# Delta-rule attention and two MoE layers on one core: GpSimd takes over five transposed copies, and the planner's costs of its inverses change

## The chip, the cores and the metric

The kernel runs on one core of a Trainium2 chip. The metric is the device time of one execution in microseconds (us); before the change the median of three runs is 900.76 us (897.88 to 901.03). TensorE is called PE, VectorE DVE, ScalarE ACT, GpSimd POOL, and SP issues the DMAs.

## The reference, cut to what matters

```python
def _attn_ref(q, k, v, beta):                    # 4 x 8 heads, 768 tokens, dim 48
    k_n = k / (np.linalg.norm(k, axis=-1, keepdims=True) + 1e-06)
    state = np.zeros((B, H, D, D))
    for t in range(S):
        y[:, :, t] = np.einsum('bhd,bhde->bhe', q[:, :, t], state)
        v_old = np.einsum('bhde,bhd->bhe', state, kt)
        state = state + bt[:, :, :, None] * np.einsum('bhd,bhe->bhde', kt, vt - v_old)
def _moe_ref(x, w_in, w_out, g_ln):              # 3072 tokens, 384 -> 1024 -> 384
    h = x @ w_in
    ...                                          # h * softmax(h), layer norm, * g_ln
    return ln @ w_out
def _moe2_ref(x, w_in, w_out):                   # 384 -> 2048 -> 384
    return (np.maximum(x @ w_in, 0.0) ** 2) @ w_out
```

The output of the attention goes through both layers.

## The kernel before, in words

The attention is computed in chunks of 64 tokens. Two chunks of eight heads each make one step t; there are 24 steps. A step needs the inverse of a unit lower triangular 64 x 64 matrix of each chunk and head. It is built from inverses of 32 x 32 blocks. The inverses of four steps (128 blocks, one on each partition) are computed together as one group, so there are six groups, g = 0 to 5 (`G0`). Group 0 is inverted on DVE, groups 1 to 5 on POOL.

The path of a group, with the lines of the profile:
- PE multiplies keys and queries (L662), ACT evicts them (L688) and SP writes them to a scratch tensor `gscr` in HBM. A chain on DVE (L790 to L799) and a small transpose on PE (L816) make the factors, which ACT evicts as `gm` (L819).
- `inversion(g, ...)` loads the blocks into a tile `it` (two of them, used in turn; order's names it_205 for odd groups and it_204 for even ones), scales them by `gm` (L891), keeps their lower triangles (L873), and then does 102 small steps: for each j a product (L910) and an addition (L927), each in one or two pieces, each depending on the one before. It ends with a memset of the diagonal (L945) and a scaling by `gm` (L952).
- `it` is written to the scratch `tscr`. A copy of it with the two block indices exchanged, `ia` (L969), is made by ACT, and written to the scratch `uscr`. From both `load_tb` fetches what a step needs.
- PE combines the blocks of step t in `prep1` (L1062, needs `tscr`) and `prep2` (L1078, needs `uscr`), and `z` (L1105), which ACT evicts as `zs` (L1119). The step itself is the products `a` (L1132, L1133), the difference r on DVE (L1148), the products `o` (L1162, L1163) and the state on DVE (L1180). `a` of step t writes the same PSUM bank as `prep1` of step t + 1 and stands behind it in PE's queue; so step 3 comes after `prep1` of step 4, the first step of group 1.
- Each step gives 128 tokens, and the first MoE layer for them fills PE's time: transposes (L1204), the first product (`p_h`, L1215), softmax and norm on DVE and ACT, transposes (`p_tr`, L1317, evicted as zh and zl, L415 and L420), and for pairs of steps the second product (`p_x`, L1337, evicted as xo, L1351). The weights are decoded from raw 64-bit words on ACT (L458, L539) and DVE (L466 to L502); the low parts `wgl` of one of them are made on POOL (L420). POOL also scales the values `vt` (L1042).
- The second MoE layer (L1480, L1524) comes last.

All queues are ordered by a planner. Every operation is recorded by `add(engine, cost, function, reads, writes, priority)`. `Plan.forward` simulates the engines with these costs and always takes, of the operations that are ready, the one with the best key; `Plan.backward` computes new keys from the same costs; the best of twelve rounds becomes the order in which the instructions are issued. Each engine executes its queue strictly in that order on the chip. A cost is a number of the planner only; it changes no instruction. `c_pool(n)` is the planner's cost of n elements on POOL, `c_act(n, True)` that of an ACT copy within SBUF: for the 1024 elements of `ia`

```python
def c_act(n, sbuf=False):
    return (0.095 if sbuf else 0.053) + n / 1200.0
```

gives 0.95 us.

Of the kernel before, what the change touches and what calls it, by code (L numbers as in the profile page):

```python
# [20 lines left out]
HB = 32  # L21
# [94 lines left out]
class Plan:  # L116
# [19 lines left out]
    def add(self, eng, cost, fn, r=(), w=(), prio=0.0, size=0, after=()):  # L136

        i = len(self.ops)
        deps = set(after)
        for k in r:  # L140
            if k in self.writer:
                deps.add(self.writer[k])
            if k in self.BANKS:

                deps.update(j for j in self.readers.get(k, ()) if self.ops[j][0] != eng)
            self.readers.setdefault(k, []).append(i)
        for k in w:
            if k in self.writer:
                deps.add(self.writer[k])
            deps.update(self.readers.get(k, ()))  # L150
            self.writer[k], self.readers[k] = i, []
        deps.discard(i)
        self.ops.append((eng, cost, fn, prio, deps, size))
        return i
# [108 lines left out]
def c_dve(n, fast=False):  # L263
    return 0.07 + n / (1920.0 if fast else 960.0)


def c_act(n, sbuf=False):
    return (0.095 if sbuf else 0.053) + n / 1200.0


def c_pool(n, full=True):

    return 0.148 + n * (2.104e-3 if full else 1.667e-3)
# [3 lines left out]
def tile_delta_moe_moe(  # L277
# [14 lines left out]
    v, act, pool, pe = nc.vector, nc.scalar, nc.gpsimd, nc.tensor  # L292
# [94 lines left out]
    ia = ap_.tile(sqr, F32, name="ia")  # L387
# [446 lines left out]

    def inversion(g, en, prio):

        eng, cost = (v, lambda n, full=True: c_dve(n) + 0.09) if en == "dve" else (pool, c_pool)
        gm = gm_[g % 2]
        it, itmp = it_[g % 2], junk[:, 512:] if g == 1 else itmp_
        kgm, kic, kia = ("A", "gm", g % 2), ("A", "itc", g % 2), ("A", "ia")  # L840
# [5 lines left out]
        n = 2 * (G0[g + 1] - G0[g])  # L846
# [54 lines left out]
        for j in range(1, HB - 1):  # L901
            nr = HB - 1 - j
            for q, (c0, c1) in enumerate(((0, min(j, s1)), (s1, j))):
                w_ = c1 - c0
                if w_ <= 0:
# [13 lines left out]
                    full=False,  # L919
# [35 lines left out]
            full=False,  # L955
# [7 lines left out]
            prio,  # L963
            P * 4096,
        )
        add(
            "act",
            c_act(HB * HB, True),
            lambda: act.copy(ia.rearrange("p s r -> p r s"), it),  # L969
            kts,  # L970
            [kia, *(kraws if g == 0 else ())],
            prio,
# [180 lines left out]
    def o_mm(t):  # L1153
        first, last = t % NCH == 0, t % NCH == NCH - 1

        def mm():
            for i in range(2):
                for p in range(NP):
                    for h in range(2):
                        s = rows[h]  # L1160
                        if not last:
                            pe.matmul(ksp[heads[h], i, p], zs_[i][s, p, C:112], R[s, i, p], start=True, stop=True)  # L1162
                        pe.matmul(  # L1163
                            xp[rows[1 - h], i, p],
                            zs_[i][s, p, 0:C],
                            R[s, i, p],
                            start=first and i == 0 and p == 0,
                            stop=True,
                            skip_group_check=True,
                        )  # L1170

        return mm, [("A", "zs", 0), ("A", "zs", 1), ("A", "r")], [("A", "a"), ("A", "o")]
# [393 lines left out]
    for t in range(T1):  # L1566
        wr = e_tile(t, -70 + t)
        norms(t, -62)
    gammas(0, -61)
    inversion(0, "dve", -55)  # L1570
    first_inv.append(plan.writer["A", "it", 0, 0])
    for t in range(T1, T2):
# [4 lines left out]

    gate.append(wr)
    inversion(1, "pool", PR["inv1"])
    load_w1i(0, 6, PR["w1i"])  # L1580
    for t in range(T2, LA):
# [16 lines left out]
    for t in range(NT + 3):  # L1598
        if t < NT:
            for g in range(2, NG):  # L1600
                if t == max(1, G0[g] - 5):
                    gammas(g, t + PR["inv"])
                    inversion(g, "pool", t + PR["inv"])
# [7 lines left out]
            parts, cost = [], 0.3  # L1611
# [23 lines left out]
            parts, cost = [o_mm(t)], 1.25  # L1635
# [113 lines left out]
```

## Time and profile before

| | |
|---|---|
| median of three runs | 900.76 us |
| profiled execution | 896.73 us |
| its span (first to last instruction) | 895.0 us |
| mean granted clock of PE (1 is 2.4 GHz, 0.5 is 1.2 GHz) | 0.96 |
| PE busy | 804.2 us (90%) |
| DVE, ACT, POOL busy | 494.7, 449.6, 311.7 us |

The span has three stages: the start until the first inverses are there, with PE often idle; the steps with the first MoE layer, to about 460 us; and the second MoE layer, where PE is busy nearly all the time. POOL works until 433 us, nearly all of it before 388 us. In a view of one engine in order of time, each line has the start, the duration of the merged instructions, the operation, and in brackets how long the engine sat idle before it and which instruction of which engine ended that.

### The profile page before, as it was taken

What the parts mean: (1) busy time and instruction counts of PE and PEld (TensorE: products, weight loads), DVE (VectorE), ACT (ScalarE), POOL (GpSimd) and SP (SyncE); (2) the same over time, 40 slices, a digit from 0 to 9 for tenths busy, and PEclk for the clock granted to TensorE, in tenths of its full rate; (3) what the DMA queues carried; (4) which work ended last, traced back from release to release, by engine and by line L of the source; (5) the groups of instructions that cost most, each with busy time, mean ns of one, the idle gap of its engine ahead of it and who ended that gap; (6) DMA issues with size and microseconds to landing.
All of it is one profiled execution on the core that took longest, in us unless ns stands there. A gap on an engine that the chain in (4) does not pass through costs nothing.

```text
span 895.0 us, 24146 instructions
## 1 busy us (share of the span) xinstructions
PE 804.2 (90%) x9904; PEld 748.0 (84%) x9904; DVE 494.7 (55%) x990; ACT 449.6 (50%) x996; POOL 311.7 (35%) x751
## 2 busy tenths in 40 slices
PE   5425759999978989999999999999999999999997
PEld 4324637888867878878889999999999999999997
DVE  5999765634974895775756444343334333343332
ACT  2315568675765675756666444343434333343333
POOL 5469989847978978920000000000000000000000
PEclk9975878999998999999999999999999999999999
DMA  9947866577687686466244311010101001010101
GB/s 243 275 119 175 251 160 172 138 158 187 176 254 190 198 204 188 145 178 182 88 130 127 112 48 53 1 54 1 53 1 38 17 1 53 1 27 1 27 1 27
DMA packets 139726, 99.71 MB, mean 111 GB/s; under 512 B 95072, under 2 KB 120672, under 8 KB 139616
## 3 DMA queue, kind: packets, MB, share of 16 engines
q1 hardware_dynamic: 139616, 98.18, 40.3%
q8 instruction: 77, 1.26, 0.6%
q14 instruction: 33, 0.27, 0.1%
HBM read 71.41 MB, written 26.74 MB: 110 GB/s over the span
## 4 chain that ended last, share of the span: by engine, by line
PE 63%; POOL 12%; DVE 7%; DMA 6%; ACT 5%; issue 3%; SPq 3%; ACTq 0%; POOLq 0%; DVEq 0%
PE acc L1524 22%; PE h L1480 22%; PE p_x L1337 7%; POOL it L927 6%; PE p_h L1215 5%; POOL junk L910 3%; SPq L300 3%; DMA raw<-in_w2i_dram 2%; POOL itmp L910 2%; PE p_tr L1317 2%; PE p_a L1132 1%; DMA m<-in_ktok_dram 1%; PE p_u L1105 1%; PE p_o L1163 1%; DVE zl L420 1%
## 5 line engine op out<-in xcount | busy, mean ns | idle before, releaser
L1501 DVE TENSOR_TENSOR xt<-xt 128x384 f32<-128x384 f32 x128 | 71.5, 558 | 167.3 <-ACT xt L1493 167.1
L1493 ACT ACTIVATE xt<-h 128x384 f32<-128x384 f32 x128 | 63.0, 492 | 167.1 <-PE h L1480 167.0
L1480 PE MATMUL h<-x1l,w2h 128*128 128x384 f32 x384 | 128.7, 335 | 0.0
L1480 PE MATMUL h<-x1h,w2h 128*128 128x384 f32 x384 | 128.6, 335 | 0.0
L1480 PE MATMUL h<-x1h,w2l 128*128 128x384 f32 x384 | 128.5, 335 | 0.0
L927 POOL TENSOR_TENSOR it<-it,itmp 128x72 f32<-128x72 f32 (+37 forms) x204 | 89.4, 454 | 4.6
L1524 PE MATMUL acc<-woh,xh 128*128 128x384 f32 x258 | 87.7, 340 | 0.7 <-ACT ot L1546 0.7
L1337 PE MATMUL p_x<-zh,wgh 128*128 128x256 f32 x288 | 86.2, 299 | 1.9 <-ACT xo L1351 1.8
L1524 PE MATMUL acc<-wol,xh 128*128 128x384 f32 x258 | 87.4, 339 | 0.0
L1524 PE MATMUL acc<-woh,xl 128*128 128x384 f32 x258 | 87.1, 338 | 0.0
L910 POOL TENSOR_TENSOR itmp<-it 128x72 f32<-128x72 f32 (+37 forms) x204 | 85.9, 436 | 2.2
L1337 PE MATMUL p_x<-zl,wgh 128*128 128x256 f32 x288 | 82.1, 285 | 0.0
L1337 PE MATMUL p_x<-zh,wgl 128*128 128x256 f32 x288 | 82.1, 285 | 0.0
L420 DVE TENSOR_TENSOR xl<-xt,xh 128x384 fp32r<-128x384 f32 x86 | 48.0, 558 | 44.7 <-ACT xh L415 44.4
L1480 PEld LDWEIGHTS h<-x1h,w2h 128*128 128x128 f32 x384 | 72.1, 188 | 0.0
L1480 PEld LDWEIGHTS h<-x1l,w2h 128*128 128x128 f32 x384 | 72.1, 188 | 0.0
L1480 PEld LDWEIGHTS h<-x1h,w2l 128*128 128x128 f32 x384 | 72.1, 188 | 0.0
L415 ACT CAST xh<-xt 128x384 fp32r<-128x384 f32 x86 | 44.1, 513 | 48.2 <-DVE xt L1501 47.0
L1215 PE MATMUL p_h<-w1h,xh 128*128 128x512 f32 x144 | 62.8, 436 | 3.3 <-DVE xl L420 3.3
L1337 PEld LDWEIGHTS p_x<-zh,wgh 128*128 128x128 f32 x288 | 55.2, 192 | 5.7 <-ACT xo L1351 2.9
L1215 PE MATMUL p_h<-w1l,xh 128*128 128x512 f32 x144 | 58.9, 409 | 0.0
L1215 PE MATMUL p_h<-w1h,xl 128*128 128x512 f32 x144 | 58.7, 408 | 0.0
(181 smaller groups left out, 1967.4 us busy)
## 6 DMA issues: line engine op xcount, KB each, us to landing
kql<-in_kin_dram SPq DMA_DIRECT2D x22, 512.0 KB, 6.5
kqe<-in_kin_dram SPq DMA_DIRECT2D x38, 192.0 KB, 6.5
raw<-in_w2i_dram SPq DMA_DIRECT2D x12, 512.0 KB, 5.2
raw<-in_w2o_dram SPq DMA_DIRECT2D x16, 384.0 KB, 4.2
gscr<-g SPq DMA_DIRECT2D x21, 256.0 KB, 4.2
m<-in_ktok_dram SPq DMA_DIRECT2D x24, 192.0 KB, 3.8
vt<-in_vtok_dram SPq DMA_DIRECT2D x24, 192.0 KB, 4.6
x1scr<-xo SPq DMA_DIRECT2D x12, 384.0 KB, 2.6
```

What stands on the lines that cost most here:

```text
L300: return add("sp", 0.06, lambda: nc.sync.dma_start(dst(), src()), r, w, prio, size, gate)
L415: add("act", c_act(n), lambda: act.copy(hi(), src()), r, [w[0]], prio)
L420: lambda: le.tensor_tensor(out=lo(), in0=src(), in1=hi().bitcast(F32), op=ALU.subtract),
L910: lambda tm=tm, j=j, nr=nr, w_=w_, c0=c0, c1=c1: eng.tensor_tensor(out=tm, in0=it[:, j + 1 :, j : j + 1].to_broadcast([P, nr, w_]), in1=it ...
L927: lambda tm=tm, j=j, c0=c0, c1=c1: eng.tensor_tensor(out=it[:, j + 1 :, c0:c1], in0=it[:, j + 1 :, c0:c1], in1=tm, op=ALU.add,),
L1215: pe.matmul(p_h[:, sl], xx[:, c], ww[:, c, sl], start=(c == 0 and k == 0), stop=(c == 2 and k == 2),)
L1317: pe.transpose(ptr[:, f], e[:, k * P : k * P + P], ident)
L1337: pe.matmul(p_x1[:, 0 : 2 * P], ww[:, f, c * P : c * P + P], zz[:, f], start=(f == 0 and k == 0), stop=(f == 7 and k == 2),)
L1480: pe.matmul(late["h2", ih], late[ww][:, c, s], xx[:, c], start=(c == 0 and k == 0), stop=(c == 2 and k == 2),)
L1493: lambda: act.activation(out=rt, in_=late["h2", ih], func=AF.Relu),
L1501: lambda: v.tensor_tensor(out=gg, in0=rt, in1=rt, op=ALU.mult),
L1524: pe.matmul(late["acc", a], gg[:, a * P : a * P + P], late[ww][:, f], start=(f == 0 and k == 0), stop=(f == 15 and k == 2),)
```

## The change

Two things. The planner reckons each step of an inverse on POOL longer: by 0.12 us in group 1, by 0.06 us in groups 2 to 5 (DVE's 0.09 us for group 0 is as before). And the copy `ia` of groups 1 to 5 is made by POOL itself (`tensor_copy`, reckoned with 1.95 us); ACT keeps that of group 0.

```diff
     def inversion(g, en, prio):
 
-        eng, cost = (v, lambda n, full=True: c_dve(n) + 0.09) if en == "dve" else (pool, c_pool)
+        eng, slow = (v, 0.09) if en == "dve" else (pool, 0.12 if g == 1 else 0.06)
+        cost = lambda n, full: (c_dve(n) if en == "dve" else c_pool(n, full)) + slow
...
+        ce, cn = (act.copy, c_act(HB * HB, True)) if g == 0 else (pool.tensor_copy, 1.95)
         add(
-            "act",
-            c_act(HB * HB, True),
-            lambda: act.copy(ia.rearrange("p s r -> p r s"), it),
+            "pool" if g else "act",
+            cn,
+            lambda: ce(ia.rearrange("p s r -> p r s"), it),
             kts,
             [kia, *(kraws if g == 0 else ())],
             prio,
```

The lines after the first edit are one further down in the changed kernel, those after the second two further (L891 is L892, L952 is L953, L969 is L971, L1062 is L1064). Because the costs feed all keys, the order changes on every engine. Three places follow.

POOL, the last steps of group 1 (it_205) and the start of group 2 (it_204). Before, from its last addition on:

```order
L927 TENSOR_TENSOR it_205<-it_205,junk 128x21
L945 MEMSET it_205 128x32
L952 TENSOR_TENSOR it_205<-it_205,gm_210 128x1024
L1042 TENSOR_TENSOR vt_189<-vt_189,nrv_185 128x384
L420 TENSOR_TENSOR wgl<-wst_217,wgh 128x384
L420 TENSOR_TENSOR wgl<-wst_218,wgh 128x384
L891 TENSOR_TENSOR it_204<-it_204,gm_209 128x1024
L873 AFFINE_SELECT it_204<-it_204 128x1024
```

Now, 24 steps before the end of group 1, and then its last rows:

```order
L928 TENSOR_TENSOR it_205<-it_205,junk 128x7x9
L941 MEMSET idle 128x16
L892 TENSOR_TENSOR it_204<-it_204,gm_209 128x1024
L911 TENSOR_TENSOR junk<-it_205 128x96
L911 TENSOR_TENSOR junk<-it_205 128x54
L928 TENSOR_TENSOR it_205<-it_205,junk 128x6x16
L928 TENSOR_TENSOR it_205<-it_205,junk 128x6x9
L941 MEMSET idle 128x16
L874 AFFINE_SELECT it_204<-it_204 128x1024
```

```order
L928 TENSOR_TENSOR it_205<-it_205,junk 128x21
L911 TENSOR_TENSOR itmp<-it_204 128x130
L946 MEMSET it_205 128x32
L928 TENSOR_TENSOR it_204<-it_204,itmp 128x26x5
L953 TENSOR_TENSOR it_205<-it_205,gm_210 128x1024
L941 MEMSET idle 128x16
L420 TENSOR_TENSOR wgl<-wst_220,wgh 128x384
L911 TENSOR_TENSOR itmp<-it_204 128x150
L971 COPY ia<-it_205 128x32x32
```

The start of group 2 (L892, which needs gm_209 from ACT, and L874) and its first ten steps now stand ahead of the end of group 1, and so do three `wgl`; the copy follows L953 with one `wgl` and one step between.

ACT, around the copy of group 1 (it_205), in the queue that also evicts z (zs_199, zs_200) and makes gm_209. Before:

```order
L1119 COPY zs_199<-p_u_221 128x448
L415 CAST xh_152<-p_h 128x384
L1258 ACTIVATE ez_157<-ez_157,sc_155 128x1024
L819 COPY gm_209<-p_u_221 128x32
L458 ACTIVATE wst_220<-raw_214 128x384
L969 COPY ia<-it_205 128x32x32
L1119 COPY zs_200<-p_u_222 128x448
```

Now:

```order
L1121 COPY zs_199<-p_u_221 128x448
L539 ACTIVATE wst_217<-wst_217,gsb 128x384
L415 CAST wgh<-wst_217 128x384
L819 COPY gm_209<-p_u_221 128x32
L539 ACTIVATE wst_218<-wst_218,gsb 128x384
L415 CAST wgh<-wst_218 128x384
L415 CAST xh_152<-p_h 128x384
L1260 ACTIVATE ez_157<-ez_157,sc_155 128x1024
L1189 COPY xt_149<-p_o 64x4x48 x4
L1121 COPY zs_200<-p_u_222 128x448
```

The copy is gone between the two evictions of z, and gm_209 stands further ahead.

POOL, the end of group 3 (it_205 again) and the start of group 4 (it_204). Before:

```order
L927 TENSOR_TENSOR it_205<-it_205,itmp 128x21
L945 MEMSET it_205 128x32
L952 TENSOR_TENSOR it_205<-it_205,gm_210 128x1024
L1042 TENSOR_TENSOR vt_189<-vt_189,nrv_184 128x384
L891 TENSOR_TENSOR it_204<-it_204,gm_209 128x1024
L873 AFFINE_SELECT it_204<-it_204 128x1024
```

Now:

```order
L928 TENSOR_TENSOR it_205<-it_205,itmp 128x21
L892 TENSOR_TENSOR it_204<-it_204,gm_209 128x1024
L946 MEMSET it_205 128x32
L874 AFFINE_SELECT it_204<-it_204 128x1024
L953 TENSOR_TENSOR it_205<-it_205,gm_210 128x1024
L911 TENSOR_TENSOR itmp<-it_204 128x30
L971 COPY ia<-it_205 128x32x32
L928 TENSOR_TENSOR it_204<-it_204,itmp 128x30
L1044 TENSOR_TENSOR vt_189<-vt_189,nrv_184 128x384
```

Here too the next group's L892 and L874 stand ahead of L953. In groups 2, 4 and 5 nothing of the next group stands ahead of L953, and the copy follows it at once or behind one vt.

On PE, between the small transpose L816 of group 2 and `prep1` of step 4, there are now 36 matmuls of `p_h` where there were 27, 24 of `p_x` where there were none, and five sets of four p_tr where there were three. Between L816 of group 4 and `prep1` of step 12, the first of group 3, there are 30 of `p_h` and 72 of `p_x` where there were 12 and 24.

## Rows read from the trace of the kernel before

**Rows 1.** The page: busy shares, and PE's busy tenths in 40 slices.

```profile
PE 804.2 (90%) x9904; PEld 748.0 (84%) x9904; DVE 494.7 (55%) x990; ACT 449.6 (50%) x996; POOL 311.7 (35%) x751
...
PE   5425759999978989999999999999999999999997
```

**Rows 2.** Windows: busy of PE, PEld, DVE, ACT, POOL; clock; DMA share; GB/s.

```profile
130.00:440.00 310.00, 288.92 (x5868) 250.76 (x5869) 206.77 (x397) 211.89 (x498) 216.55 (x567) 0.96 0.66 180
...
280.00:300.00 20.00, 19.52 (x356) 17.29 (x357) 11.10 (x19) 11.94 (x32) 17.25 (x45) 0.83 0.68 191
```

**Rows 3.** ACT in order of time, around its copies of groups 1, 3 and 5.

```profile
116.26 0.18 ACT L819 COPY gm<-p_u 128x32 f32<-128x32 f32 x1
...
123.74 1.93 ACT L969 COPY ia<-it 128x1024 f32<-128x1024 f32 x1 [6.84 <-POOL it L952]
...
255.36 0.67 ACT L458 ACTIVATE wst<-raw 128x512 f32<-128x512 f32 x1 [4.15 <-DMA raw<-in_w2i_dram]
255.99 1.96 ACT L969 COPY ia<-it 128x1024 f32<-128x1024 f32 x1
...
385.55 2.04 ACT L969 COPY ia<-it 128x1024 f32<-128x1024 f32 x1 [3.70 <-POOL it L952]
```

**Rows 4.** PE in order of time, the instructions that it waited for.

```profile
67.35 0.74 PE L1062 MATMUL p_a<-tbd,g 32*32 32x32 f32 x32 [16.41 <-DMA tbd<-tscr]
...
126.09 1.57 PE L662 MATMUL p_u<-kqe 48*64 48x128 f32 x28 [3.13 <-ACT zs L1119]
...
130.31 1.12 PE L1317 MATMUL p_tr<-ident,ez 128*128 128x128 f32 x4 [2.65 <-DVE zl L420]
...
139.27 0.65 PE L1062 MATMUL p_a<-tbd,g 32*32 32x32 f32 x32
...
258.56 0.26 PE L816 MATMUL p_u<-ident,be 32*32 32x32 f32 x8 [3.09 <-ACT zs L1119]
...
280.48 1.11 PE L1317 MATMUL p_tr<-ident,ez 128*128 128x128 f32 x4 [2.41 <-ACT ez L1258]
...
388.04 0.39 PE L1337 MATMUL p_x<-zh,wgh 128*128 128x256 f32 x1 [0.96 <-ACT xo L1351]
```

**Rows 5.** POOL in order of time: end of group 1, start of group 2.

```profile
107.03 0.88 POOL L910 TENSOR_TENSOR junk<-it 128x96 f32<-128x96 f32 x2
...
109.62 0.99 POOL L420 TENSOR_TENSOR wgl<-wst,wgh 128x384 fp32r<-128x384 f32 x1
...
117.00 3.61 POOL L927 TENSOR_TENSOR it<-it,junk 128x40 f32<-128x40 f32 x1
...
121.79 1.91 POOL L952 TENSOR_TENSOR it<-it,gm 128x1024 f32<-128x1024 f32 x1
...
128.54 2.36 POOL L891 TENSOR_TENSOR it<-it,gm 128x1024 f32<-128x1024 f32 x1
130.97 1.27 POOL L873 TENSOR_SCALAR_AFFINE_SELECT it<-it 128x1024 f32<-128x1024 f32 x1
132.32 0.25 POOL L910 TENSOR_TENSOR itmp<-it 128x30 f32<-128x30 f32 x1
...
139.62 0.66 POOL L927 TENSOR_TENSOR it<-it,itmp 128x130 f32<-128x130 f32 x1
```

**Rows 6.** DVE in order of time beside 117.00, and POOL's groups by form (busy, mean ns).

```profile
117.60 1.01 DVE L477 SCALAR_TENSOR_TENSOR wst<-wst,cst 128x384 uint32<-128x384 uint32 x2
...
L927 POOL TENSOR_TENSOR it<-it,itmp 128x40 f32<-128x40 f32 x8 | 2.5, 309 | 0.0
```

**Rows 7.** SP in order of time: from the copy of group 0 to the loads.

```profile
62.85 1.41 SPq L300 DMA_DIRECT2D uscr<-ia  x2
64.36 2.19 SPq L300 DMA_DIRECT2D tbd<-tscr  x4
```

**Rows 8.** The chain in order of time: PE's fillers.

```profile
164.72 2.88 PE p_x L1337 x24
...
170.87 2.09 PE p_h L1215 x9
```

## The prediction

> **What bounds the kernel now.** I read the page first, then windows, then each engine in order of time around the six copies `ia`. The page shows PE busy for 804.2 of 895.0 us, and its slices show where the rest is: digits of 2 to 7 at the start, mostly 9 from the seventh slice on, with an 8 or a 7 here and there [rows 1]. So the last stage can't get faster by this change, since PE alone sets it, and what the change can win or lose is PE's idle time in the first 460 us. In the 310 us from 130 to 440 PE is busy for 288.9 us; some 21 us are idle there [rows 2]. A wait costs more than itself where the clock falls: from 280 to 300 us the granted clock is 0.83 of 2.4 GHz, right behind a stall of 2.41 us at 280.48, which is 6.8 us at 1.2 GHz (0.17 / 0.5 x 20), in which PE did 3.4 us less than at 2.4 GHz [rows 2, 4].
>
> ACT in order of time shows what the copies do there. Its copy of group 1 stands in the queue from 116.9 on and waits 6.84 us for POOL, then runs 1.93 us; in group 5 it waits 3.70 us and runs 2.04 [rows 3]. All that stands behind it on ACT waits too. PE shows who feels it: at 126.09 it had waited 3.13 us for an eviction of z (zs) that stood behind the copy, and at 130.31 2.65 us for the low parts zl, which come from evictions further back in the same queue; at 258.56 it had waited 3.09 us for a zs behind the copy of group 3, and at 388.04 0.96 us for an xo behind that of group 5 [rows 3, 4]. The planner reckoned 0.95 us for a copy that takes 1.93 to 2.04, and it thought the inverses shorter than they are, so it put the copy where the chip isn't ready for it.
>
> **What the planner's numbers do.** A cost by itself runs nothing longer. What counts is the new order, and two consequences of it. First, with an inverse that ends later in the plan, the next group's start is ready before that end, and the planner slips it in: on POOL the start of group 2 now stands 24 steps ahead of the end of group 1, and the start of group 4 ahead of L953 of group 3. Second, PE has more of the first MoE layer ahead of the first `prep1` of groups 1 and 3.
>
> **The sum, against the profiled execution's 896.73 us.**
>
> (a) ACT no longer stands for group 1. The waits for zs and zl, 3.13 + 2.65 [rows 4], go: -5.8 us. What is late next is `prep1` of step 4, (b). Bounds: -5.8, or nothing if zl is late for DVE's own work.
>
> (b) Group 1 ends later, and behind `prep1` of step 4 stands `a` of step 3. PE reached that `prep1` at 139.27 without having to wait [rows 4]. Without the 5.8 us of (a) it would be there at 133.5; ahead of it are now 9 more of p_h (2.09 us), 24 more of p_x (2.88 us) [rows 8] and two more sets of p_tr (up to 1.11 each [rows 4]), together 7.2 us: 140.7. That work isn't lost, it is done earlier. POOL: the start of group 2 needs gm, which was evicted by 116.44 [rows 3]; now that it stands ahead of an activation on ACT I take 115.4. L892 and L874 take 2.36 + 1.27 us [rows 5]: 119.0. The last 24 steps of group 1 took from 107.03 to 121.79, less three operations of other tiles at 0.99 us: 11.8 us; one of them took 3.61 us where eight of the same size average 0.309 [rows 5, 6], so 8.5 without that accident; I take 10.1. Three `wgl` now among them: 3.0. The first ten steps of group 2: they took from 132.32 to 140.28, with two `wgl` in between, so 6.0 at most, and I take 5.0, since part of it fills gaps between dependent steps. L953: 1.9. That makes 139.0 for the end of the inverse (135.4 to 142.7 with the ends of each). Then one `wgl`, one step and the copy.
>
> The copy on POOL is in no trace of before. Bounds: 1.27 us (L873, one input, the same 1024 elements) and 2.36 (L891, two inputs). I take 1.9, near L952's 1.91 and ACT's own 1.93 to 2.04 [rows 3, 5]. The Trainium skill's GPSIMD Engine Reference, section Elementwise — side-by-side cycle accounting, holds a loop with one input to be bound by its port at 1.03 cycles per element; by that the copy would be about 0.9 us, an estimate from the page's 1.2 GHz, and the sum 1.0 us lower. No row shows a copy, and L873 is nearest to it.
>
> The copy ends at 139.0 + 1.0 + 0.5 + 1.9 = 142.4. From the end of group 0's copy, where SP issues the write of uscr and then the loads, `prep1` followed after 67.35 - 62.85 = 4.5 us [rows 4, 7]. SP's queue has the same order now: both writes of uscr stand ahead of the loads, so the copy holds the loads as well. `prep1` of step 4 can start at 146.9, and PE waits 6.3 us for it: +6.3, bounds +2.7 and +10. What (a) gives, (b) takes back.
>
> (c) ACT's copy of group 3 no longer stands between the load wait at 255.36 and zs: -2.0 of the 3.09 us at 258.56 [rows 3, 4]. The end of group 3 is later by L892 and L874, 3.6 us, by the wait for gm, and by the copy; what hides it is 18 more of p_h and 48 more of p_x ahead of `prep1` of step 12, 2 x 2.09 + 2 x 2.88 = 9.9 us [rows 8]. If that cover were too short, the rest would be lost on PE.
>
> (d) The xo of group 5 no longer waits behind the copy: -1.0 [rows 3, 4].
>
> (e) The stall at 280.48 was a p_tr ahead of `o` of step 11; in the new queue that p_tr isn't there, and the step's products go first. I take the 2.41 us and half of the 3.4 us that the clock cost: -4.1. Bounds 0 (another wait takes its place) and -5.8.
>
> (f) POOL has five copies more, 9.5 us, and what stands behind a copy there (a `vt`, the next group's steps) is late by one. For groups 1 and 3 that is in (b) and (c); for 2, 4 and 5 the bounds are 0 and 3 x 1.9 = 5.7 us, and I take +1.0, since PE is seldom at the very edge of an inverse: before, it waited for a load of `tscr` once, at 67.35 [rows 4].
>
> Sum: -5.8 + 6.3 - 2.0 - 1.0 - 4.1 + 1.0 = **-5.6 us**, 891.1 us for an execution like the profiled one. The median shown, 900.76, is 4.0 us above that one; the forecast for a median is 900.76 - 5.6 = **895.2 us**. About 0.5%, 4.5 us, is what a measurement of this kernel can tell from no change.
>
> **Rivals.**
>
> 1. Slower: POOL's queue makes group 1 late. Its last 24 steps stand behind L892, which can't start before ACT has evicted gm; the ten steps and the `wgl` follow; and the copy reads SBUF beside a busy DVE. For it speaks the step at 117.00: 3.61 us instead of 0.309, while DVE ran its decoding (L477 and its like, two inputs from SBUF) one after another [rows 6]. If the copy is held as that step was, it is 3.3 us longer; with (b) at its upper end `prep1` starts at 150.6 + 3.3 = 153.9, and PE waits 13.2 instead of 6.3 us: +6.9. Then steps 3 to 5 have to go on without the filler that was spent before, 2 x 2.88 us: +5.8. Together -5.6 + 12.7 = +7.1, so 907.9 us. It decides from a copy of group 1 that ends after about 147. Against it: the accident was one step of some hundred in that group. The Trainium skill's page SBUF — State Buffer, section Who interferes with whom, has this as a rule: a DVE instruction with two SBUF inputs and a GpSimd instruction that reads SBUF exclude each other, and the later one waits for the whole of the other, while ScalarE never waits. It speaks against this move; by it rival 1's 3.3 us are no accident. The trace agrees for the one step; in the rows of L891 and L952 it is not to be seen.
>
> 2. No change: the waits move. ACT had waited 4.15 us for a load of w2 at 255.36 before it came to the copy [rows 3]; with the copy gone that wait remains, (c) gives 1 us only, and (e) finds another stall: -5.8 + 6.3 - 1.0 - 1.0 + 0 + 1.0 = -0.5, 900.3 us.
>
> 3. Better: the planner's times fit the chip now, (b) is at its lower end and (e) whole, and POOL's copies cost nothing: -5.8 + 2.7 - 2.0 - 1.0 - 5.8 = -11.9, 888.9 us.
>
> **How the numbers follow.** Forecast 0.34, rival 3 0.14, rival 2 0.32, rival 1 0.20. The forecast and rival 3 are faster by over 0.5% (below 896.3), together 0.48; rival 2 is within 0.5%, 0.32; rival 1 is slower, 0.20. The forecast's own range is 890 to 899, by (b)'s bounds. The range is 885 to 908: below rival 3 by what the copy's lower bound and small waits could add, and up to rival 1.
>
> **What would show it.** Right: no wait of ACT for POOL's L953 beside group 0's; POOL's copies at 1.9 us; group 1's inverse ending near 139 and its copy near 142; PE waiting some 6 us at `prep1` of step 4, none at zs near 126 and less than 1.5 us at the small transpose of group 4; the clock from 280 to 300 above 0.9. Wrong: a copy near 5 us, an end of group 1 after 147, or a PE that waits more than 22 us in all from 130 to 440.

## The result, and the profile after

The change makes the kernel slower by about 1%: 907.73 us, the median of five runs (900.83 to 910.35), against 898.36 us for the kernel before on the same chip, also the median of five (897.11 to 901.03). The ratio is 1.0098, with a 95% interval of 1.0069 to 1.0127. All figures here and below are of fast runs; the one slow run, 2024.09 us in e6, is left out. The forecast was 895.2 us; the result lies at the upper edge of its range (885 to 908) and on the side of its first rival (907.9 us). The profiled execution of the change took 905.39 us (span 903.5), 8.7 us more than that of before (896.73).

The page of the change, its busy line and PE's slices, for [rows 1]:

```profile
PE 813.8 (90%) x9904; PEld 757.8 (84%) x9904; DVE 497.5 (55%) x990; ACT 440.3 (49%) x991; POOL 318.9 (35%) x756
...
PE   5435788999889999998999999999999999999997
```

The same number of matmuls keeps PE busy 9.6 us longer; the mean granted clock of the span is 0.951 instead of 0.96. Windows (columns as in [rows 2]) say where; first the kernel before, with stretches that were not shown ahead:

```profile
0.00:130.00 130.00, 68.41 (x1262) 54.90 (x1262) 102.75 (x273) 53.74 (x137) 95.15 (x185) 0.82 0.75 201
130.00:180.00 50.00, 46.47 (x946) 39.07 (x947) 31.33 (x66) 37.88 (x94) 44.59 (x126) 0.90 0.63 167
180.00:400.00 220.00, 203.59 (x4048) 177.61 (x4046) 148.96 (x282) 146.64 (x341) 169.24 (x439) 0.97 0.70 188
400.00:440.00 40.00, 38.86 (x887) 34.07 (x878) 26.49 (x52) 27.37 (x64) 2.71 (x3) 1.00 0.52 151
```

Then the change:

```profile
0.00:130.00 130.00, 73.00 (x1281) 59.03 (x1282) 113.53 (x288) 59.12 (x152) 96.80 (x192) 0.81 0.77 207
130.00:180.00 50.00, 44.78 (x939) 38.99 (x938) 23.29 (x51) 32.30 (x77) 43.40 (x125) 0.91 0.62 159
180.00:400.00 220.00, 205.09 (x3956) 179.34 (x3954) 147.50 (x259) 137.95 (x336) 175.80 (x439) 0.96 0.67 185
400.00:440.00 40.00, 33.46 (x691) 28.71 (x690) 20.58 (x58) 20.51 (x49) 2.69 (x3) 0.83 0.55 152
...
280.00:300.00 20.00, 20.00 (x493) 17.51 (x490) 11.62 (x21) 10.58 (x32) 11.14 (x25) 1.00 0.74 188
```

Up to 130 us PE did more than before, from 130 to 400 about the same, and from 400 to 440 it was idle 6.5 us instead of 1.1 and ran at 0.83 of full speed instead of 1.00, which is another 5.7 us (0.17 x 33.46): about 11 us, more than this execution lost in all. That is the first step of group 5 and the steps behind it. On PE, in order of time, the longer waits of the change around group 1, behind the small transpose of group 4, and in that last stretch:

```profile
122.73 0.66 PE L1319 MATMUL p_tr<-ident,ez 128*128 128x128 f32 x4 [1.71 <-DVE zl L420]
...
124.64 0.69 PE L1206 MATMUL p_h<-ident,xt 128*128 128x128 f32 x3 [1.25 <-DVE ez L1250]
...
139.24 1.12 PE L1319 MATMUL p_tr<-ident,ez 128*128 128x128 f32 x4 [2.84 <-ACT ez L1260]
...
142.04 0.64 PE L1064 MATMUL p_a<-tbd,g 32*32 32x32 f32 x30 [0.16 <-DMA tbd<-tscr]
...
263.07 0.58 PE L1339 MATMUL p_x<-zh,wgh 128*128 128x256 f32 x1 [4.45 <-ACT xo L1353]
...
418.69 0.90 PE L1206 MATMUL p_h<-ident,xt 128*128 128x128 f32 x3 [3.83 <-ACT xt L1189]
...
432.09 0.34 PE L1134 MATMUL p_a<-s,kql 48*64 48x48 f32 x1 [1.91 <-ACT ys L1070]
```

The `prep1` of step 4 waits 0.16 us for its data, not the 6.3 of the forecast: PE comes to it at 141.57, since a `p_tr` and 24 `p_x` stand in front and that `p_tr` waits 2.84 us for ACT's `ez`. POOL in order of time, the ends of groups 1, 3 and 5 and a `vt` in the middle of group 4:

```profile
112.63 2.65 POOL L892 TENSOR_TENSOR it<-it,gm 128x1024 f32<-128x1024 f32 x1
...
132.46 1.91 POOL L953 TENSOR_TENSOR it<-it,gm 128x1024 f32<-128x1024 f32 x1
...
135.79 1.98 POOL L971 COPY ia<-it 128x1024 f32<-128x1024 f32 x1
...
253.45 2.41 POOL L892 TENSOR_TENSOR it<-it,gm 128x1024 f32<-128x1024 f32 x1 [6.69 <-DMA m<-in_ktok_dram]
...
257.51 2.33 POOL L953 TENSOR_TENSOR it<-it,gm 128x1024 f32<-128x1024 f32 x1
...
291.14 1.09 POOL L1044 TENSOR_TENSOR vt<-vt,nrv 128x384 f32<-128x384 f32 x1 [8.75 <-DMA vt<-in_vtok_dram]
...
391.89 1.91 POOL L953 TENSOR_TENSOR it<-it,gm 128x1024 f32<-128x1024 f32 x1
```

Group 1 ends at 134.4 (before 123.7, [rows 5]). Group 4's L892 waits 6.69 us in front of the end of group 3. The bracket names a load, but what came last is `gm`, on ACT:

```profile
253.19 0.19 ACT L819 COPY gm<-p_u 128x32 f32<-128x32 f32 x1
```

Group 5's L953 starts at 391.89, in the kernel before at 383.60. Where that lateness begins is told by r, the difference of a step on DVE, which marks the chain of steps. Here is r of step 8 (the first of group 2) and of step 11, before and then in the change:

```profile
216.67 0.55 DVE L1148 TENSOR_TENSOR r<-vt,p_a 128x384 f32<-128x384 f32 x1 [0.48 <-PE p_a L1078]
...
273.66 0.56 DVE L1148 TENSOR_TENSOR r<-vt,p_a 128x384 f32<-128x384 f32 x1
```

```profile
215.62 0.55 DVE L1150 TENSOR_TENSOR r<-vt,p_a 128x384 f32<-128x384 f32 x1 [0.50 <-PE p_a L1080]
...
282.56 0.55 DVE L1150 TENSOR_TENSOR r<-vt,p_a 128x384 f32<-128x384 f32 x1 [4.43 <-PE p_o L1135]
```

r of step 3 is 3.9 us late (147.82 instead of 143.95), but step 8 is 1.0 us early, and so is group 2's L953 (182.03 instead of 182.85): by then this execution had made the late group 1 good, and r of step 10 is 3.0 us early (244.64 instead of 247.67). r of step 11 is 8.9 us late. SP loads the next `vt`, whose tile must have been read first, at 285.01 instead of 277.49, POOL waits 8.75 us for it at 291.14, group 4's L953 starts at 324.64 instead of 319.00, and group 5's is 8.3 us late. The steps 13 to 16 are level with before again (r of step 16 at 351.07 instead of 350.94); POOL's lateness stays, and r of step 19 is 8.8 us late (409.25 instead of 400.46).

### The profile page after: what moved, and what is told of

The parts are those of the page before. It is cut to its first block, busy times and chain, and to the rows that moved or that the text cites. A ratio compares the mean times of both kernels' runs of the same rounds, so it can differ in the third digit from the quotient of the medians.

```text
span 903.5 us, 24159 instructions
## 1 busy us (share of the span) xinstructions
PE 813.8 (90%) x9904; PEld 757.8 (84%) x9904; DVE 497.5 (55%) x990; ACT 440.3 (49%) x991; POOL 318.9 (35%) x756
## 4 chain that ended last, share of the span: by engine, by line
PE 66%; DMA 9%; DVE 8%; POOL 8%; ACT 4%; issue 3%; SPq 2%; ACTq 0%; POOLq 0%; DVEq 0%
PE h L1482 22%; PE acc L1526 22%; PE p_x L1339 7%; PE p_h L1217 7%; POOL it L928 3%; POOL itmp L911 2%; SPq L300 2%; PE p_a L1134 2%; DMA gscr<-g 1%; DMA m<-in_ktok_dram 1%; DVE it L928 1%; PE p_tr L1319 1%; DVE wst L466 1%; DVE itmp L911 1%; DMA raw<-in_w2o_dram 1%
## 5 line engine op out<-in xcount | busy, mean ns | idle before, releaser
L911 POOL TENSOR_TENSOR itmp<-it 128x72 f32<-128x72 f32 (+37 forms) x204 | 88.8, 450 | 1.7
L928 POOL TENSOR_TENSOR it<-it,itmp 128x72 f32<-128x72 f32 (+37 forms) x204 | 84.5, 429 | 4.0
```

Of the source, the lines that this page charges most:

```text
L911: lambda tm=tm, j=j, nr=nr, w_=w_, c0=c0, c1=c1: eng.tensor_tensor(out=tm, in0=it[:, j + 1 :, j : j + 1].to_broadcast([P, nr, w_]), in1=it ...
L928: lambda tm=tm, j=j, c0=c0, c1=c1: eng.tensor_tensor(out=it[:, j + 1 :, c0:c1], in0=it[:, j + 1 :, c0:c1], in1=tm, op=ALU.add,),
```

## The experiments

Ratios are to the kernel before in the same session (895.57 to 898.63 us), with 95% intervals; each kernel ran 4 to 12 times. The code of an edit is shortened where it is longer than a line. r of a step is again its difference on DVE.

### Which half of the change

e1 is the kernel before with the first edit of the change, e2 with the second. e3 is the kernel before with its order, in which POOL issues the copies; e4 the change with its order, in which ACT issues them:

```diff
 e3
-            lambda: act.copy(ia.rearrange("p s r -> p r s"), it),
+            lambda: (pool.tensor_copy if g else act.copy)(ia.rearrange("p s r -> p r s"), it),
 e4
-            lambda: ce(ia.rearrange("p s r -> p r s"), it),
+            lambda: act.copy(ia.rearrange("p s r -> p r s"), it),
```

Theory A: the order spends `p_x` ahead of step 20 that is missing later; Theory B: the copies on POOL make the inverses late; Theory C: group 5's inverse ends late.

> Only the planner's longer costs of the inverses' steps; ACT makes all copies as before. Theory A (the new order spends the first layer's p_x ahead of prep1 of step 20, 24 here and 48 in the change, none before; steps 19 to 22 then run without filler): slower than before by 3 to 10 us, with idle and a low clock of PE between 400 and 435 us. Theory B (the copies on POOL make the inverses late): within 0.3% of before, as no copy has moved.

> Only the move of five copies to POOL, reckoned with 1.95 us; the steps' costs as before. Its order has no p_x between the last p_h and prep1 of step 20, as before. Theory A: within 0.5% of before or up to 5 us faster. Theory B: slower by 5 to 10 us, as the change.

> The order of before on every engine, only that POOL issues the five copies at the place where the planner had put them for ACT. Theory A: within 0.5% of before, or faster by the 5 to 8 us that PE waited behind ACT's copies (zs near 126 and 258 us, xo near 388). Theory B: slower by 5 us or more.

> The order of the change on every engine, only that ACT issues the five copies at the place where the planner had put them for POOL. Theory A: slower than before as the change is, 6 to 13 us, since the order is the change's and ACT waits for POOL again. Theory B: within 0.5% of before.

Measured: e1 908.93 us, 1.0127 (1.0098 to 1.0156); e2 893.64, 0.9973 (0.9948 to 0.9997); e3 897.78, 1.0006 (0.9981 to 1.0031); e4 909.01, 1.0144 (1.0111 to 1.0177). The costs lose all of it. The copies on POOL cost nothing that can be told (e3), and planned by themselves they gain 0.3%, with an interval that ends just below 1 (e2). Theory B falls.

### Which part of the new order: first tries

```diff
-        eng, slow = (v, 0.09) if en == "dve" else (pool, 0.12 if g == 1 else 0.06)
 e6
+        eng, slow = (v, 0.09) if en == "dve" else (pool, (0, 0.12, 0.06, 0.06, 0.06, 0)[g])
 e7
+        eng, slow = (v, 0.09) if en == "dve" else (pool, 0.12 if g == 1 else 0)
 e8
+        eng, slow = (v, 0.09) if en == "dve" else (pool, 0.06 if g == 5 else 0)
```

e5 keeps the change's costs and moves instructions of its order by hand: 48 `p_x` ahead of `prep1` of step 20 and 24 behind it, with all that depends on them, are held until the products of steps 19 to 21 named here have gone out:

```diff
+        late = sorted((i for i in px if pos[i] < first), key=pos.get)[-8:]
+        late += sorted((i for i in px if pos[i] > first), key=pos.get)[:4]
+        goal = dict(zip(late, [mark["a", 19]] * 2 + [mark["o", 19]] * 2 + [mark["a", 20]] * 4 + [mark["o", 20]] * 2 + [mark["a", 21]] * 2))
```

> The order of the change, except that the 48 p_x ahead of prep1 of step 20 and the 24 behind it are put back among steps 19 to 22 (12 after a of step 19, 12 after o of step 19, 24 after a of step 20, 12 and 12 later), with what depends on them. Theory A (filler spent too early): the loss goes, within 0.5% of before (893 to 901 us), r of step 19 near 401 us, and the softmax of the twentieth tile near 420 us instead of 429. Theory C (the inverse of group 5 itself ends 8 us later, so prep1 of step 20 is late whatever stands before it): PE waits at that prep1 and the time stays within 3 us of the change's (904 to 911).

> The change with the longer costs in groups 1 to 4 only; the copy of group 5 stays on POOL. The planner then puts no p_x ahead of prep1 of step 20. Theory A: no loss, 890 to 899 us. Theory C: the same, if the inverse of group 5 ends near 386 us as before, else as slow as the change.

> The change with the 0.12 us of group 1 kept and no longer costs in groups 2 to 5. No p_x ahead of prep1 of step 20. Theory A: 890 to 899 us; whether the longer cost of group 1 by itself gains or loses is read against the copy-only kernel's 893.6.

> The change with a longer cost (0.06 us) in group 5 alone; 18 p_x ahead of prep1 of step 20. Theory A: the loss is there, if smaller: 3 to 8 us slower than the copy-only kernel's 893.6, r of step 19 at 405 us or later.

Measured: e5 924.96 us, 1.0311 (1.0276 to 1.0346); e6 914.35, 1.0187 (1.0138 to 1.0236); e7 908.32, 1.0104 (1.0056 to 1.0151); e8 894.29, 0.9963 (0.9938 to 0.9988). Spreading the `p_x` made it much worse. In e6, between `prep1` of step 19 and that of step 20, PE has no more `p_x` than in the kernel before (72; the change has 120), and it is slower than the change: Theory A falls. Theory C isn't settled: group 5's L953 starts at 400.90 in e5 and at 395.57 in e6, later than in the change. The 0.12 us of group 1 alone are enough for the loss; the 0.06 us of group 5 alone lose nothing, and can't be told from e2.

### One queue of the change put back

`queue` is the planned order of one engine, `inv[g]` the instructions of group g's inverse; `merged` issues that queue and leaves the others as planned. e9 (g = 3) and e10 (g = 1) on POOL, e11 on ACT (n is the first eviction of step 19), e14 with POOL's order of e2 (`short`), and e15 with e10's edit and five PE instructions held until `a` of step 3:

```diff
-        for i in plan.order():
 e9, e10
+        early = [i for i in queue[:end] if i in inv[g + 1]]
+        queue = [i for i in queue[:end] if i not in early] + early + queue[end:]
+        for i in merged(order, queue):
 e11
+        queue = queue[: n - 1] + queue[n : n + 8] + queue[n - 1 : n] + queue[n + 8 :]
 e14
+        for i in merged(long, short, ("pool",)):
 e15
+        back = sorted((i for i in px if pos[i] < pos[mark[1, 4]]), key=pos.get)[-5:]
+        goal = dict.fromkeys(back, mark["a", 3])
```

Theory D: group 1's late end on POOL decides. G: L892 of group 4 in front of the end of group 3 decides. E: the load in front of `xt` decides. Q: POOL's queue as a whole. P1, P2: PE's order ahead of step 4, or of each group's first step.

> The change, with one edit of POOL's queue alone: the memset, L953 and the copy of group 3 stand ahead of L892 and L874 of group 4 again, as before the change; the queues of PE, DVE, ACT and SP are the change's, row for row. Theory G: in the change L892 of group 4 waits 6.69 us for gm in front of the end of group 3, which so ends at 259.8 (L953 at 257.51) where its last step was done near 246.7, and every later group is late by it (group 5's L953 at 391.89 against 383.60 before). G expects L953 of group 3 to start at 246 to 250, that of group 5 at 383 to 387, and 897 to 902 us. Theory D (group 1's late end decides) and Theory E (a load that ACT waits for in front of the eviction of step 19 decides) both expect no change: 905 to 910 us.

> The change, with one edit of POOL's queue alone: L892, L874 and the first ten steps of group 2 stand behind the copy of group 1, as they did before the change; the other queues are the change's, row for row. Theory D (group 1 ends 11 us later than before, and that lateness is never made good) expects L953 of group 1 at 118 to 124 instead of 132.5 and 896 to 902 us. Theory G expects the earlier end (118 to 124) to buy nothing, since PE didn't wait for group 1 in the change, and group 2, which starts later, to end 2 to 6 us later: 905 to 911 us.

> The change, with one edit of ACT's queue alone: the decoding step L458 that waited 3.65 us for its load at 416.79, in front of the evictions of step 19's result (xt), ys and z, stands behind these eight instructions. Theory E (this wait, PE's wait of 3.83 us at 418.69 that follows from it and the fall of the clock to 0.74 and 0.66 from 420 to 440 are the loss) expects PE's wait at that xT under 1 us, a clock above 0.95 from 410 to 440 and 895 to 900 us. Theory G expects only the wait itself to go: 902 to 907 us.

> The queues of PE, DVE, ACT and SP are the change's, row for row; the queue of POOL is that of the kernel with the copies only (893.6 us), row for row. Theory Q expects 893 to 899 us. Theories P1 and P2 (PE's queue is what loses) expect 903 to 909 us, and that PE still comes to prep1 of step 4 after 140 although group 1 ends near 120.

> The change with its order back at one place: on POOL the start of group 2 stands behind the copy of group 1 (as in e10), and on PE one set of p_tr and 24 p_x that stood ahead of prep1 of step 4 stand behind a of step 3; all else in the change's order. Theory P1 expects prep1 of step 4 at 133 to 138, r of step 3 at 139 to 144 and 894 to 900 us. Theories P2 and Q expect the gain to be lost again later: 901 to 907 us.

Measured: e9 904.70 us, 1.0096 (1.0058 to 1.0134); e10 905.11, 1.0114 (1.0092 to 1.0136); e11 906.29, 1.0120 (1.0097 to 1.0142); e14 911.24, 1.0136 (1.0112 to 1.0161); e15 910.93, 1.0134 (1.0108 to 1.0160). None gains what its theory wanted, though the edits do what they say. In e9 group 3's end starts at 247.86 instead of 257.51, but group 5's at 391.83 as before the edit, since r of step 11 (284.52) and POOL's wait for a `vt` (8.56 us at 291.06) are as late as they were; in e11 the wait at `xT` is gone, but PE's clock from 420 to 440 is 0.83 (0.70 in the change), where Theory E wanted it above 0.95. D, G, E and Q fall as single causes inside the change. Why group 1's earlier end doesn't reach the steps is seen in e14, POOL and then SP in order of time, and PE:

```profile
116.55 2.16 POOL L958 TENSOR_TENSOR it<-it,gm 128x1024 f32<-128x1024 f32 x1
```

```profile
122.58 7.88 SPq L300 DMA_DIRECT2D raw<-in_w2i_dram  x2
...
139.79 1.98 SPq L300 DMA_DIRECT2D raw<-in_w2i_dram  x2
141.86 0.38 SPq L300 DMA_DIRECT2D tscr<-it  x1
```

```profile
150.47 0.28 PE L1069 MATMUL p_a<-tbd,g 32*32 32x32 f32 x2 [0.56 <-DMA tbd<-tscr]
```

The inverse is done at 118.7, but its write to `tscr` stands on SP behind loads of raw weights that are issued as late as 139.79 and goes out at 141.86; `prep1` of step 4 starts at 150.47. In e2 the write is issued at 120.39. In e14 PE comes to that `prep1` at 149.9 only, since it had waited for `ez` ahead of it; in e15 PE's wait is all for the inverse, done at 125.9 and written at 136.52 (SP, then PE):

```profile
136.52 0.38 SPq L300 DMA_DIRECT2D tscr<-it  x1
```

```profile
145.33 0.28 PE L1070 MATMUL p_a<-tbd,g 32*32 32x32 f32 x2 [6.72 <-DMA tbd<-tscr]
```

The plan for a late inverse is in every queue, not in POOL's alone. In e10, e14 and e15 `prep1` of step 4 comes at 145.73, 150.47 and 145.33, later than in the change (141.57), so they don't show what an earlier step 3 would be worth there.

### One part alone, in the fast kernel

All three are e2 with one move. In e12 `head` is L891 and L873 of group 4, `tail` the memset, L952 and the copy of group 3; in e17 (t = 12 and 20) and e18 (t = 4) `prep1` of step t and what depends on it are held until four sets of six `p_x` more have gone out:

```diff
 e12
+        queue = rest[:n] + [head[0], tail[0], head[1], *tail[1:]] + rest[n:]
 e17, e18
+            first = mark[1, t]
+            goal[first] = sorted((i for i in px if pos[i] > pos[first]), key=pos.get)[3]
```

> The kernel in which only the copies are on POOL (893.6 us), with one edit of POOL's queue alone: L891 and L873 of group 4 stand ahead of the memset and ahead of L952 of group 3, as in the change; all other queues stay. Theory G expects L891 to wait some 5 to 8 us for gm in front of the end of group 3, L952 of group 3 at 255 to 259 instead of 249.0, and a loss of 3 to 9 us: 897 to 903 us. Theories D and E expect 891 to 896 us, since group 1 and ACT's queue are untouched.

> The kernel with the copies only (893.6 us); prep1 of step 12 and what depends on it stand behind the next 24 p_x, 9 p_h and one set of p_tr on PE, and prep1 of step 20 behind the next 24 p_x, 18 p_h and two sets of p_tr, as the longer costs place it. Nothing else moves. Theory P2 (a first step of a group behind more filler loses, since the steps are a chain that then starts later and has no filler left) expects r of step 11 at 276 to 281 instead of 273.0, r of step 19 at 399 to 406 instead of 393.3, and 897 to 903 us. Theory R (the order of fillers is neutral, since PE has the same work in all; the loss lies elsewhere in the plan) expects 891 to 896 us.

> The kernel with the copies only; prep1 of step 4 and what depends on it (a of step 3 and so step 3) stand behind the next 15 p_h, one set of p_tr and 24 p_x on PE, as the longer cost of group 1 places it. Nothing else is changed. P2 expects r of step 3 at 144 to 150 instead of 138.1 and 898 to 906 us (the run with the longer cost in group 1 alone: 908.3). R expects 891 to 896 us.

Measured: e12 898.32 us, 1.0037 (1.0023 to 1.0050); e17 896.45, 0.9986 (0.9966 to 1.0006); e18 903.99, 1.0085 (1.0055 to 1.0114). With e2 at 0.9973, e18 costs 1.1%, e12 0.6%, and e17 nothing that can be told (0.1%, give or take 0.3%). So all the filler that the change has ahead of the first step of group 1 loses by itself. e17 is a weaker test than its text says: it puts 24 `p_x` more ahead of steps 12 and 20, where the change's trace has 48 more than e2's ahead of each. With that half, r of step 11 is 3.7 us later than in e2 (276.72 instead of 273.03; in the change it is 9.5 us later) and r of step 19 10.3 us (403.60 instead of 393.29), as P2 expected, but group 5's inverse is only 1.4 us later and the time can't be told from e2's (e17, DVE and then POOL, group 5; e2's starts at 380.82):

```profile
276.72 0.55 DVE L1151 TENSOR_TENSOR r<-vt,p_a 128x384 f32<-128x384 f32 x1 [2.68 <-PE p_o L1136]
```

```profile
382.24 1.92 POOL L954 TENSOR_TENSOR it<-it,gm 128x1024 f32<-128x1024 f32 x1
```

How e18 loses: first the copies-only kernel, PE's `prep1` of step 4, r of step 3 on DVE, then POOL (each fence in order of time):

```profile
133.81 0.65 PE L1063 MATMUL p_a<-tbd,g 32*32 32x32 f32 x32
```

```profile
138.05 0.55 DVE L1149 TENSOR_TENSOR r<-vt,p_a 128x384 f32<-128x384 f32 x1 [0.73 <-PE p_o L1134]
```

```profile
148.01 0.83 POOL L1043 TENSOR_TENSOR vt<-vt,nrv 128x384 f32<-128x384 f32 x1
...
157.82 0.83 POOL L1043 TENSOR_TENSOR vt<-vt,nrv 128x384 f32<-128x384 f32 x1
...
173.46 0.83 POOL L1043 TENSOR_TENSOR vt<-vt,nrv 128x384 f32<-128x384 f32 x1 [2.14 <-DMA vt<-in_vtok_dram]
...
179.14 1.91 POOL L952 TENSOR_TENSOR it<-it,gm 128x1024 f32<-128x1024 f32 x1
...
380.82 1.92 POOL L952 TENSOR_TENSOR it<-it,gm 128x1024 f32<-128x1024 f32 x1
```

Then e18, the same instructions, with the wait of PE that makes it later still:

```profile
142.92 0.39 PE L1340 MATMUL p_x<-zh,wgh 128*128 128x256 f32 x1 [4.20 <-ACT zh L415]
...
146.75 0.65 PE L1065 MATMUL p_a<-tbd,g 32*32 32x32 f32 x32
...
149.43 0.30 PE L1135 MATMUL p_a<-s,kql 48*64 48x48 f32 x1
```

```profile
150.24 0.56 DVE L1151 TENSOR_TENSOR r<-vt,p_a 128x384 f32<-128x384 f32 x1 [5.98 <-POOL idle L942]
```

```profile
150.82 0.33 SPq L300 DMA_DIRECT2D vt<-in_vtok_dram  x1
```

```profile
154.75 0.83 POOL L1045 TENSOR_TENSOR vt<-vt,nrv 128x384 f32<-128x384 f32 x1 [4.62 <-DMA vt<-in_vtok_dram]
...
166.92 0.83 POOL L1045 TENSOR_TENSOR vt<-vt,nrv 128x384 f32<-128x384 f32 x1 [5.25 <-DMA vt<-in_vtok_dram]
...
182.30 0.83 POOL L1045 TENSOR_TENSOR vt<-vt,nrv 128x384 f32<-128x384 f32 x1 [1.90 <-DMA vt<-in_vtok_dram]
...
187.98 1.91 POOL L954 TENSOR_TENSOR it<-it,gm 128x1024 f32<-128x1024 f32 x1
...
392.02 1.91 POOL L954 TENSOR_TENSOR it<-it,gm 128x1024 f32<-128x1024 f32 x1
```

It is a loop. `prep1` of step 4 comes 12.9 us later, and so r of step 3 12.2 us. (The bracket at r names a memset of POOL, which r doesn't need; r needs the products `a` of step 3, the last of which starts at 149.43.) The tile `vt` (two, used in turn) is loaded again only when that r has read it, at 150.82; POOL comes to the scaling of `vt` in the middle of group 2's inverse and waits 4.62 and then 5.25 us. Group 2 ends 8.8 us later, and the lateness is handed on from group to group: group 5's L952 is 11.2 us late, and r of step 23 stands at 461.2 instead of 453.5. The work that PE did early doesn't win the time back here, since the steps and POOL's inverses wait for each other. e17's late steps miss this loop: the late step 11 held up no inverse (group 4's L952 starts at 314.39, in e2 at 314.22), and behind step 19 there is none left to be late. e12 enters the loop at another place. Group 4's start waits 5.48 us for `gm`, and L952 of group 3 starts at 259.89 instead of 249.03, that of group 5 at 386.41 instead of 380.82:

```profile
255.85 2.39 POOL L894 TENSOR_TENSOR it<-it,gm 128x1024 f32<-128x1024 f32 x1 [5.48 <-ACT gm L819]
```

### The costs apart, and the other direction

```diff
-        eng, slow = (v, 0.09) if en == "dve" else (pool, 0.12 if g == 1 else 0.06)
 e13
+        eng, slow = (v, 0.09) if en == "dve" else (pool, 0 if g == 1 else 0.06)
 e16
+        eng, slow = (v, 0.09) if en == "dve" else (pool, -0.03)
```

> The change with no longer cost in group 1, and 0.06 us in groups 2 to 5 as in the change. Its order ahead of prep1 of step 4 is again like that of the kernel with the copies only (9 of p_h, no p_x, no p_tr more), while ahead of prep1 of step 12 stand 66 p_x and ahead of that of step 20 36 (change: 72 and 60; copies only: 24 and 12). Theory P1 (the order ahead of step 4 is the loss) expects 890 to 896 us. Theory P2 (each first step of a group that is put behind more filler loses) expects 898 to 904 us. Theory Q (GpSimd's queue loses, by instructions of others that stand too early among the steps) expects 900 to 907 us, as there the start of group 4 is ahead of the end of group 3 too.

> The change with the planner's cost of every step of an inverse on POOL 0.03 us shorter than c_pool instead of longer. Ahead of prep1 of step 4 stand fewer instructions on PE than in any of the other orders, ahead of that of step 12 18 p_x and of step 20 12. P1, P2 and Q all expect it to be as fast as the kernel with the copies only or a little faster: 888 to 895 us. If the longer costs lost only because any other order than the tuned one is worse, it comes out at 898 to 908 us.

Measured: e13 903.86 us, 1.0075 (1.0047 to 1.0103); e16 895.84, 0.9967 (0.9949 to 0.9985). P1 falls as the only cause: without group 1's cost most of the loss is there. In e13 POOL waits 5.36 us ahead of a `vt` at 181.97, and the start of group 3 (183.87) stands ahead of the end of group 2, whose L953 starts at 191.55 (e2: 179.14). What of this loses isn't shown. e12's mechanism, a start ahead of an end, is one candidate, but it was shown at one place only. The filler ahead of step 12 is another: e13 has 42 `p_x` more there than e2 and its r of step 11 is at 281.40, and e17 tried 24.

e2, e8 and e16 beat both kernels, at 0.9973, 0.9963 and 0.9967; their intervals overlap, and none is better than the others by these runs.

One row goes with the time in all twenty profiled executions, the start of group 5's last scaling by `gm` (L952 before, L953 in the change), as Theory C would have it: where it lies from 380.82 to 386.71 us (before, e2, e3, e7, e8, e12, e16, e17), they took 891.71 to 899.93 us, and where it lies from 391.83 to 404.29 us (the other twelve), 898.06 to 927.79 us. That they go together doesn't show which is the cause.

## Why the prediction was wrong

- **(a), zs and zl, -5.8.** The zs wait is gone as said, and ACT no longer stands for POOL's L953. But PE's waits from 118 to 142 are 1.71, 1.25 and 2.84 us and smaller ones: one of them again for zl, and the longest for `ez`, which the text didn't list. In all PE waited 6.7 us there instead of 7.6, so 0.9 of the 5.8 us were gained.
- **(b), group 1, +6.3.** The inverse ended at 134.4, below its lower bound of 135.4 (which the terms given don't add up to), and the copy at 137.77 instead of 142.4, since `gm` was evicted at 109.76 and L892 started at 112.63 instead of 115.4. PE waited 0.16 us instead of 6.3. The step that failed is the sentence "That work isn't lost, it is done earlier": the filler ahead of `prep1` of step 4 was counted as free. e18 puts it at 1.1%, some 10 us, in the kernel with the copies only, by its delay of step 3. r of step 3 came at 147.82 in the change, against 143.95 before and 138.05 in e2. But the profiled execution made that good, against the kernel before by step 8 and against e2 by step 10 (r at 244.64, in e2 at 244.73); the lateness that lasted in it came under (c), where the same step failed.
- **(c), group 3, -2.0.** The wait for zs at the small transpose is gone, but PE waits 4.45 us for an xo at 263.07 in its stead. And the "9.9 us" of cover were again filler ahead of a step: r of step 11 is at 282.6 instead of 273.7, POOL waited 6.69 us for `gm` and then 8.75 at 291.14 for a `vt`, and group 5's inverse ended 8.3 us late. By e17 half of such filler alone is free at this place; all of it was not tried. The wait for `gm` in front of the end of group 3, which the text named and didn't price, is what e12 finds to cost 0.6%; undone in the change (e9), it gains nothing that can be told. How the loss in the change is shared between these stays open.
- **(d)** The wait for xo is gone; one for zl of 1.52 us stands at 394.22 in its stead.
- **(e), -4.1.** Right: from 280 to 300 the clock is 1.00 and PE busy all the time [rows 2]. But the sum had no term for the stretch from 400 to 440 us, where about 11 us were lost.
- **(f), the copies.** Right in price: 1.98, 2.10, 1.93, 2.08 and 2.07 us against 1.9; the estimate of 0.9 us from the Trainium skill's GPSIMD Engine Reference (Elementwise — side-by-side cycle accounting) is too low by half. Of the +1.0 taken e3 shows nothing, but its interval (0.9981 to 1.0031) would hide it.
- **The signs.** ACT waits for no L953 but group 0's, and the copies and the clock from 280 to 300 are as said. PE's idle time from 130 to 440 is 26.7 us (310 less 44.78, 205.09 and 33.46), above the 22 that the text gave as a sign of being wrong.
- **Rival 2**'s "the waits move" is what (a), (c) and (d) show; the loss beyond them it didn't have.
- **Rival 1** had the sign. That its 907.9 us meet the 907.73 measured is luck: of its added 12.7 us, 6.9 are a wait of PE at `prep1` of step 4, which was 0.16 us. The copy wasn't held, and it ended well before 147, the point from which the rival was to decide. None of the 25 copies on POOL in the profiles of the change, e2, e8, e9 and e12 took more than 2.53 us, where the step at 117.00 had taken 3.61 [rows 5]; the rule of the Trainium skill's page SBUF — State Buffer (Who interferes with whom) shows in none of them by more than 0.6 us. The rival's sentence on steps 3 to 5, which must go on without the filler that was spent, isn't borne out: the change was level with the kernel before again at step 8.

The chance of 0.48 for faster rested on a sum of PE's waits. Such a sum sees what a queue waits for, and not that a step put later can make the next inverse late. It had no term for the chain of steps, which in the change's profile ended 13.8 us late (r of step 23 at 463.98 instead of 450.22).

## What to carry to other kernels

Where two chains hand work to each other (here the steps on PE and DVE, and the inverses on POOL), cost a new order by when the handing points come (r of a step, the end of an inverse), not by PE's waits: in e18 filler put ahead of the first handing point delayed every later one, while in e17 filler ahead of the last one, behind which no inverse follows, cost nothing that could be told. A planner's cost nearer to the chip's duration isn't by that a better cost, since it moves all five queues; price its order, not its numbers, and try one cost at a time: here group 1's alone lost, and group 5's alone made no difference that could be told. Putting one queue back in a plan that was laid out for a late inverse recovered nothing that could be told in four tries (e9, e10, e11, e14); what was late then stood in another queue, in e14 in SP's.

## What was not expected of the hardware

- A copy of 128 x 1024 fp32 with its two inner indices exchanged took 1.93 to 2.10 us on POOL in the change, and 1.93 to 2.12 on ACT before (groups 1 to 5): no dearer on POOL.
- The same order may lose in different places. The change lost its time from 400 to 440 us; e11, whose queues are the same, row for row, up to 416 us, had r of step 3 at 152.39 instead of 147.82. The 12.2 us of e18 are well beyond that scatter; the 3.9 us by which the change is behind the kernel before at step 3 are not. The executions of one order also differ: e7 ran from 899.82 to 911.91 us, the change from 900.83 to 910.35, e16 from 892.75 to 898.41, and some profiles, as those of e7 and e9, are of the fastest run of their kernel (899.82 and 898.06 us; medians 908.32 and 904.70). So a single profile doesn't show where such an order loses; here it pointed to 400 to 440 us, and the tries there (e5, e11) found nothing.
